# First pass: adding the output products' results into SBUF by VectorE in place of accumulating DMAs

## The chip, the cores and the metric

The kernel runs on one core of one Trainium2 chip. A core has a matrix engine (TensorE, PE in the rows; PEld is its loading of weights), VectorE (DVE), ScalarE (ACT), GpSimd (POOL), a sync engine that issues transfers (SP), and 16 DMA engines that all its transfers share. The metric is the device time of one execution in microseconds, the median of the runs shown; lower is better.

## What is computed

```python
def _attn_ref(q, k, v):                       # 4 batches, 12 heads, 448 x 64
    scores = scale * np.matmul(q, k.transpose(0, 1, 3, 2)) - np.log(S)
    attn = 1.0 / (1.0 + np.exp(-scores))
    return np.matmul(attn, v).astype(np.float32)
...
x = attn_out.transpose(0, 2, 1, 3).reshape(1792, 768)
h = x @ moe_w_in;  x = (h - np.tanh(h)) @ moe_w_out          # 768 -> 2048 -> 768
h = x @ moe2_w_in; r = np.maximum(h, 0.0)
out = (s * (r * r) + b) @ moe2_w_out
```

All is float32. The four weight matrices arrive as 64-bit floats.

## The kernel before, in words

**Products.** Every product is made of three TensorE passes over a high and a low part of each operand. Both parts are made on the chip: a copy rounds the source to the high part (by ScalarE or VectorE) and a VectorE subtraction gives the low part. `hi_lo` (lines 644 to 646) does it for weights (tile `w`), `half` (526 to 529) for the layers' inputs (tile `xo`).

**Passes.** The program makes two passes, each over two batches (896 rows of x). A pass is the attention of 12 pairs of heads and then two layers (`Layers.run`). In the trace the first pass ends near 543 us, and the attention of the second pass follows it, up to about 620 us. A layer takes its 2048 hidden columns in four groups of 512, numbered 0 to 3 (`grp`). In each group the first product fills g, and the output product multiplies g by the group's rows of the second weight matrix and adds to the layer's output: `out1` in layer 0 (12 PSUM banks of 128x448 in each group) and `out2` in layer 1 (14 banks of 128x384). The output lives in SBUF under the name `y`.

**Adding up, first pass.** In `out1` and `out2` the function `evict` empties each bank. Group 0 copies it into `y` (ScalarE or VectorE). Groups 1 and 2 go through `add_on` (1128 to 1133): a copy from PSUM into one of four `t` tiles, and then an accumulating DMA, issued by GpSimd, that adds `t` to `y`. Group 3 is added by VectorE from PSUM into `y`. In the second pass another function adds by accumulating DMAs into `acc` in DRAM; the change doesn't touch it.

**Weights, first pass.** SP loads 768 KB of 64-bit words (`raw`). Four steps (a scaling, then three of VectorE) turn them into 32-bit `wf`, and `keep` (625 to 632) has SP store each `wf` to DRAM, 384 KB (`win`, `wout`), for the second pass, which loads them back. Sums of weight blocks are made in place in `wf`, so they wait for that store to have read the tile. Then `hi_lo` splits into `w`.

**Order.** The program isn't written in the order in which engines run it. `Plan` (lines 88 to 235) collects operations with an assumed time on each engine (busy, and until done) and lists them: TensorE's order stays as written, and for VectorE, ScalarE, GpSimd and SP it takes in turn what is ready by those assumed times and due first. An operation marked EITHER goes to ScalarE or VectorE as the list finds it. The engines then run their lists strictly in that order. So a changed number, or a removed operation, can move others far from the place of the edit.

All instructions carry line 85 in the rows (a helper), so rows are told apart by tiles. `hs`, `two` and `one` are PSUM banks, `af` the attention weights, `qt` and `kt` the parts of q and k, `rawqkv` what is loaded for them.

Of the kernel before, what the change touches and what calls it, by code (L numbers as in the profile page):

```python
# [19 lines left out]
def tile_kernel(ctx, tc, q, k, v, w_in1, w_out1, w_in2, w_out2, s_in, b_in, out):  # L20
# [504 lines left out]

    def half(nm, j, src, keys, sbuf=True):
        t, key, _ = xo[nm, j]
        do(EITHER, (0.46, 0.35 if sbuf else 0.54), lambda e: copy(e, t()[:, 0], src()), r=keys, w=[(*key, 0)])
        do("DVE", 0.54, lambda: dve.tensor_tensor(out=t()[:, 1], in0=src(), in1=t()[:, 0].bitcast(F32), op=ALU.subtract), r=[*keys, (*key, 0)], w=[(*key, 1)])

    def less(o, a, b, r, w):
# [41 lines left out]
    class Layers:  # L573
# [52 lines left out]
        def keep(self, k, key):  # L626

            def fn():
                scratch[key] = dram.tile([P, WE], F32, name="w" + "_".join(map(str, key)))
                sp.dma_start(out=scratch[key], in_=f_t[k])  # L630

            self.do("SP", (1.9, 3.0), fn, r=[("f", k)], w=[("d", key)])

        def kept_sums(self, key):
            return key[1] == 0 and key[2] < (FG if key[0] == "in" else 2)
# [6 lines left out]
            return self.f_of.pop(n)  # L642

        def hi_lo(self, src, hi, lo, r, w, half=False):
            self.do(EITHER, (0.42, 0.3) if half else (0.74, 0.47), lambda e: copy(e, hi(), src), r=r, w=[w[0]])
            self.do("DVE", 0.47 if half else 0.88, lambda: dve.tensor_tensor(out=lo(), in0=src, in1=hi().bitcast(F32), op=ALU.subtract), r=[*r, w[0]], w=[w[1]])

        def w_whole(self, k):

# [475 lines left out]
            prod("3", "a", 1)  # L1125
            to("a", 0, 1, True)

        def add_on(self, bank, m, to, keys):

            k = self.t.take()  # L1130
            self.do(EITHER, (0.43, 0.54) if m == S else (0.38, 0.47), lambda e: copy(e, self.tt[k][:, :m], self.banks[bank][:, :m]), r=[("b", bank)], w=[("t", k)])
            self.do("POOL", (1.0, 7.0), lambda: pool.dma_start(out=to(), in_=self.tt[k][:, :m], accum_op=ALU.add), r=[("t", k)], w=keys)
            self.t.give(k)

        def out1(self, layer, grp, n, close):

            final = grp == FC // FG - 1
            ps = {}

            def y(hd, d, fs):  # L1140
                for i in range(2):
                    if fs[0] == 0:
                        ps[hd, d, i] = self.b.take()
                for f in fs:
                    for i in range(2):
                        kh, kl = self.units[n + 2 * hd + f // 2]
                        o = slice(f % 2 * HM + d * P, f % 2 * HM + d * P + P)
                        bank = ps[hd, d, i]

                        def fn(kh=kh, kl=kl, o=o, f=f, i=i, bank=bank):  # L1150
                            p, x, xs = self.banks[bank], g_t[f], slice(i * S, i * S + S)
                            pe.matmul(p, self.wt[kh][:, o], x[:, 0, xs], start=f == 0, stop=False)
                            pe.matmul(p, self.wt[kh][:, o], x[:, 1, xs], start=False, stop=False)
                            pe.matmul(p, self.wt[kl][:, o], x[:, 0, xs], start=False, stop=f == FG - 1)

                        self.do("PE", 0.608, fn, r=[("w", kh), ("w", kl), ("g", f, i, 0), ("g", f, i, 1)], w=[("b", bank)])

            def evict(hd, d):
                dm = hd * 3 + d
                t = lambda i: ys_t["y"][dm][:, i]  # L1160
                yk = [cells(dm * T2 + i * S, S) for i in range(2)]
                for i in range(2):
                    bank = ps[hd, d, i]
                    if grp == 0:
                        self.do(EITHER, (0.43, 0.54), lambda e, bank=bank, i=i: copy(e, t(i), self.banks[bank]), r=[("b", bank)], w=yk[i])
                    elif not self.sb and 0 < grp < FC // FG - 1:
                        self.add_on(bank, S, lambda i=i: t(i), yk[i])
                    else:
                        self.do("DVE", 0.54, lambda bank=bank, i=i: dve.tensor_tensor(out=t(i), in0=self.banks[bank], in1=t(i), op=ALU.add), r=[("b", bank)], w=yk[i])
                    self.b.give(bank)  # L1170
                if d == 2:
                    for k in range(2):
                        self.w_done(*self.units.pop(n + 2 * hd + k))
                if not final:
                    return
                j = dm // 2
                p = self.tt
                if dm % 2 == 0:
                    k = self.y_t1 = self.t.take()
                    half("11", j, lambda: t(0), yk[0])  # L1180
                    less(lambda: p[k], lambda: t(1), lambda: t(0), [*yk[0], *yk[1]], [("t", k)])
                    half("t1", j, lambda: p[k], [("t", k)])
                    return
                k1, k2, k3, k4 = self.y_t1, *(self.t.take() for _ in range(3))
                b11, bk = (lambda: ys_t["y"][dm - 1][:, 0]), cells((dm - 1) * T2, S)
                half("21", j, lambda: t(0), yk[0])
                less(lambda: p[k2], lambda: t(1), lambda: p[k1], [*yk[1], ("t", k1)], [("t", k2)])
                half("t2", j, lambda: p[k2], [("t", k2)])
                less(lambda: p[k3], lambda: p[k2], b11, [("t", k2), *bk], [("t", k3)])
                half("t3", j, lambda: p[k3], [("t", k3)])  # L1190
                half("22", j, lambda: t(1), yk[1])
                less(lambda: p[k4], lambda: t(0), lambda: p[k2], [("t", k2), *yk[0]], [("t", k4)])
                half("t4", j, lambda: p[k4], [("t", k4)])
                for k in (k1, k2, k3, k4):
                    self.t.give(k)

            for k in range(2):
                self.w_out(n + k)
            y(0, 0, (0, 1))
            now(close)  # L1200
            y(0, 1, (0, 1))
            y(0, 2, (0, 1))
            for d in range(3):
                y(0, d, (2, 3))
                evict(0, d)
            for k in range(2, 4):
                self.w_out(n + k)
            for d in range(3):
                y(1, d, range(FG))
                evict(1, d)  # L1210

        def out2(self, layer, grp, n, close):
# [24 lines left out]
            def evict(hd, t):  # L1237
# [2 lines left out]
                ks = cells(t * DM + hd * HM, HM)  # L1240
                if grp == 0:
                    self.do(EITHER, (0.38, 0.47), lambda e: copy(e, zt(), self.banks[bank][:, :HM]), r=[("b", bank)], w=ks)
                elif not self.sb and 0 < grp < FC // FG - 1:
                    self.add_on(bank, HM, zt, ks)
                else:
                    self.do("DVE", 0.47, lambda: dve.tensor_tensor(out=zt(), in0=self.banks[bank][:, :HM], in1=zt(), op=ALU.add), r=[("b", bank)], w=ks)
                self.b.give(bank)
# [136 lines left out]
```

## Time and profile before

| what | us |
|---|---|
| median of the runs shown | 1054.42 |
| the runs | 1052.88, 1054.45, 1054.42 |
| the profiled execution | 1049.27 |
| span of that execution in the trace | 1047.5 |
| TensorE busy in it | 1028.0 |
| VectorE busy in it | 892.0 |
| ScalarE busy in it | 601.1 |

A busy time is the time in which at least one instruction of the engine was under way. A window view gives that time for a stretch, beside the granted TensorE clock (1.00 is 2.4 GHz, 0.50 is 1.2 GHz, a mean lies between) and the mean share of the DMA engines that were busy. A timeline view gives single instructions with the idle time ahead of them in brackets, and what ended it. The chain of waits leads back from the last instruction, at each step to what released it.

### The profile page before, as it was taken

The page shows a single profiled execution, that of the slowest core. Times are in us where ns is not written, and L with a number is a line of the kernel's source. Part 1 is how long each engine was busy: PE and PEld are TensorE (multiplying, and loading weights), DVE is VectorE, ACT ScalarE, POOL GpSimd, SP SyncE. Part 2 cuts the span into 40 slices and gives each one's busy share as a digit, 9 for nine tenths or more (in the row PEclk, how much of TensorE's full clock was granted, in tenths as well). Part 3 has the DMA queues.
Part 4 walks back from the last instruction along what each step waited for, and adds up shares of the span by engine and source line. Part 5 has one row for each costly group of instructions (what it writes and reads, how often), then busy time and mean ns, then how long its engine had stood idle before and what let it go on. Part 6 is the DMA issues. An engine that isn't in the chain of part 4 may idle for free.

```text
span 1047.5 us, 15848 instructions
## 1 busy us (share of the span) xinstructions
PE 1028.0 (98%) x5688; PEld 896.7 (86%) x5688; DVE 892.0 (85%) x1480; ACT 601.1 (57%) x990; POOL 187.9 (18%) x238
## 2 busy tenths in 40 slices
PE   8999999999999999899999899999999999999998
PEld 4557999898988999898985459999999999999998
DVE  4899989897999998898856689798887999898962
ACT  5776666464555665454426566656555466666650
POOL 4220001203000003122222100306060003061600
PEclk9999999999999999999999999999999999999999
DMA  6773567969722659879576503929497019293963
GB/s 154 201 189 121 166 198 208 281 193 276 213 71 98 187 178 231 235 196 284 137 227 152 179 16 123 233 92 213 104 224 215 31 38 225 80 211 84 214 170 106
DMA packets 137966, 176.92 MB, mean 169 GB/s; under 512 B 53760, under 2 KB 108800, under 8 KB 137888
## 3 DMA queue, kind: packets, MB, share of 16 engines
q1 hardware_dynamic: 111200, 135.82, 41.6%
q0 software_dynamic: 25888, 39.89, 22.0%
q8 instruction: 45, 0.74, 0.3%
q10 hardware_dynamic: 800, 0.20, 0.1%
q14 instruction: 33, 0.27, 0.1%
HBM read 103.02 MB, written 61.83 MB: 157 GB/s over the span
## 4 chain that ended last, share of the span: by engine, by line
PE 76%; DVE 14%; DMA 5%; issue 2%; ACT 1%; SPq 0%; DVEq 0%; ACTq 0%
PE hs L85 64%; PE two L85 6%; PE one L85 6%; DVE t L85 4%; DVE wf L85 3%; DVE w L85 2%; DVE raw L85 2%; DVE xo L85 1%; DVE g L85 1%; DMA win<-wf 1%; DMA raw<-in_moe_w_out_dram 1%; DVE y L85 1%; DMA raw<-in_moe_w_in_dram 1%; DMA wf<-wout 1%; ACT t L85 1%
## 5 line engine op out<-in xcount | busy, mean ns | idle before, releaser
L85 PE MATMUL hs<-xo,w 128*128 128x448 f32 x2016 | 423.7, 368 | 6.6 <-DVE t L85 5.7
L85 PEld LDWEIGHTS hs<-xo,w 128*128 128x128 f32 x2016 | 378.2, 188 | 45.5 <-DVE t L85 7.6
L85 PE MATMUL hs<-w,g 128*128 128x384 f32 x1290 | 228.1, 335 | 0.7 <-DVE w L85 0.6
L85 PE MATMUL hs<-g,w 128*128 128x448 f32 x1098 | 226.4, 366 | 0.0
L85 PEld LDWEIGHTS hs<-w,g 128*128 128x128 f32 x1290 | 224.1, 188 | 2.2 <-DVE w L85 0.9
L85 PEld LDWEIGHTS hs<-g,w 128*128 128x128 f32 x1098 | 206.1, 188 | 17.2 <-DVE g L85 0.3
L85 DVE TENSOR_TENSOR w<-wf,w 128x768 fp32r<-128x768 f32 (+1 forms) x216 | 187.7, 883 | 23.5 <-PE hs L85 11.9
L85 ACT COPY t<-hs 128x448 f32<-128x448 f32 (+2 forms) x239 | 120.1, 515 | 111.1 <-PE hs L85 99.8
L85 ACT CAST w<-wf 128x768 fp32r<-128x768 f32 (+1 forms) x177 | 137.2, 781 | 77.5 <-DVE wf L85 58.5
L85 POOL DMA_DIRECT2D acc<-t x106 | 93.6, 1227 | 318.0 <-ACT t L85 157.1
L85 POOL DMA_DIRECT2D y<-t x52 | 46.1, 985 | 371.0 <-ACT t L85 177.4
L85 DVE TENSOR_TENSOR g<-t,g 128x448 fp32r<-128x448 f32 (+2 forms) x170 | 98.6, 596 | 6.7 <-ACT g L85 6.1
L85 DVE TENSOR_TENSOR wf<-wf 128x384 f32<-128x384 f32 x168 | 93.3, 556 | 12.6 <-DMA win<-wf 7.4
L85 ACT CAST g<-t 128x448 fp32r<-128x448 f32 (+2 forms) x147 | 79.9, 552 | 33.4 <-DVE t L85 31.7
L85 ACT ACTIVATE af<-two,nlogs 128x896 f32<-128x896 f32 (+1 forms) x96 | 85.2, 919 | 8.5 <-PE two L85 6.2
L85 DVE TENSOR_TENSOR t<-hs,t 128x448 f32<-128x448 f32 x114 | 70.2, 619 | 6.2 <-PE hs L85 4.1
L85 ACT ACTIVATE raw<-raw 128x768 f32<-128x768 f32 x60 | 55.6, 926 | 33.3 <-DMA raw<-in_moe_w_out_dram 23.4
L85 DVE SCALAR_TENSOR_TENSOR raw<-raw 128x768 uint32<-128x768 uint32 x64 | 61.2, 957 | 5.5 <-ACT raw L85 3.7
L85 ACT ACTIVATE t<-t,b_sb,s_sb 128x448 f32<-128x448 f32 x64 | 48.0, 761 | 25.4 <-DVE t L85 25.1
L85 DVE TENSOR_TENSOR t<-t 128x448 f32<-128x448 f32 (+1 forms) x98 | 58.8, 603 | 4.1 <-ACT t L85 3.8
L85 DVE SCALAR_TENSOR_TENSOR wf<-raw 128x768 uint32<-128x768 uint32 x64 | 60.7, 953 | 0.7
L85 PE MATMUL two<-qt,kt 64*128 64x448 f32 x396 | 51.4, 384 | 0.1
(79 smaller groups left out, 710.8 us busy)
## 6 DMA issues: line engine op xcount, KB each, us to landing
raw<-in_moe_w_in_dram SPq DMA_DIRECT2D x32, 768.0 KB, 5.7
raw<-in_moe_w_out_dram SPq DMA_DIRECT2D x32, 768.0 KB, 7.9
wf<-wout SPq DMA_DIRECT2D x36, 384.0 KB, 6.6
win<-wf SPq DMA_DIRECT2D x32, 384.0 KB, 3.5
wout<-wf SPq DMA_DIRECT2D x32, 384.0 KB, 6.3
wf<-win SPq DMA_DIRECT2D x32, 384.0 KB, 4.3
acc<-t POOLq DMA_DIRECT2D x51, 224.0 KB, 7.7
acc<-t POOLq DMA_DIRECT2D x55, 192.0 KB, 8.0
```

The source lines that it names most:

```text
L85: return lambda *a, **kw: tc.keep_in_program_order(getattr(self.engine, name)(*a, **kw))
```

## The change

It does two things. In the first pass `evict` adds the banks of groups 1 and 2 by VectorE too, straight from PSUM into `y`, as group 3 does, and `add_on` is gone. And four assumed times of the list are raised: VectorE's copy in `half`, `keep`'s time until done, VectorE's half-width copy in `hi_lo`, and the half-width subtraction there.

```diff
     def half(nm, j, src, keys, sbuf=True):
         t, key, _ = xo[nm, j]
-        do(EITHER, (0.46, 0.35 if sbuf else 0.54), lambda e: copy(e, t()[:, 0], src()), r=keys, w=[(*key, 0)])
+        do(EITHER, (0.46, 0.38 if sbuf else 0.6), lambda e: copy(e, t()[:, 0], src()), r=keys, w=[(*key, 0)])
...
-            self.do("SP", (1.9, 3.0), fn, r=[("f", k)], w=[("d", key)])
+            self.do("SP", (1.9, 5.2), fn, r=[("f", k)], w=[("d", key)])
...
-            self.do(EITHER, (0.42, 0.3) if half else (0.74, 0.47), lambda e: copy(e, hi(), src), r=r, w=[w[0]])
-            self.do("DVE", 0.47 if half else 0.88, lambda: dve.tensor_tensor(out=lo(), in0=src, in1=hi().bitcast(F32), op=ALU.subtract), r=[*r, w[0]], w=[w[1]])
+            self.do(EITHER, (0.42, 0.5) if half else (0.74, 0.47), lambda e: copy(e, hi(), src), r=r, w=[w[0]])
+            self.do("DVE", 0.52 if half else 0.88, lambda: dve.tensor_tensor(out=lo(), in0=src, in1=hi().bitcast(F32), op=ALU.subtract), r=[*r, w[0]], w=[w[1]])
...
-        def add_on(self, bank, m, to, keys):
-
-            k = self.t.take()
-            self.do(EITHER, (0.43, 0.54) if m == S else (0.38, 0.47), lambda e: copy(e, self.tt[k][:, :m], self.banks[bank][:, :m]), r=[("b", bank)], w=[("t", k)])
-            self.do("POOL", (1.0, 7.0), lambda: pool.dma_start(out=to(), in_=self.tt[k][:, :m], accum_op=ALU.add), r=[("t", k)], w=keys)
-            self.t.give(k)
...
-                    elif not self.sb and 0 < grp < FC // FG - 1:
-                        self.add_on(bank, S, lambda i=i: t(i), yk[i])
...
-                elif not self.sb and 0 < grp < FC // FG - 1:
-                    self.add_on(bank, HM, zt, ks)
```

TensorE's order is the same in both programs. By the instruction lists GpSimd issues 52 transfers fewer (24 of 128x448 in layer 0, 28 of 128x384 in layer 1). VectorE has 36 instructions more and ScalarE 36 fewer. On VectorE the adds of `hs` into `y` go from 26 to 50 at 448 columns and from 14 to 42 at 384; its copies `t<-hs` go from 26 to 18 and from 17 to 8; its 768-wide rounding copies `w<-wf` go from 31 to 39; the rest shifts by a few either way. SP has 440 transfers in both.

The order on VectorE at three places follows; the numbers in the names are those of tile buffers and differ between the programs.

The first place is layer 0, group 2: VectorE while weights of the next group are made and the banks of group 1 are emptied (177 to 200 us in the trace of before). Before:

```order
L85 SCALAR_TENSOR_TENSOR raw_105<-raw_105 128x768
L85 SCALAR_TENSOR_TENSOR wf_84<-raw_105 128x768
L85 TENSOR_TENSOR w_996<-wf_83,w_992 128x768
L85 TENSOR_TENSOR w_79<-wf_84,w_79 128x384
L85 TENSOR_SCALAR raw_106<-raw_106 128x768
L85 SCALAR_TENSOR_TENSOR raw_106<-raw_106 128x768
L85 TENSOR_TENSOR wf_84<-wf_84 128x3x128
```

VectorE at the same place in the changed program:

```order
L85 SCALAR_TENSOR_TENSOR raw_105<-raw_105 128x768
L85 SCALAR_TENSOR_TENSOR wf_84<-raw_105 128x768
L85 TENSOR_TENSOR y_140<-hs_957,y_140 128x448
L85 TENSOR_TENSOR y_140<-hs_963,y_140 128x448
L85 TENSOR_TENSOR y_140<-hs_959,y_140 128x448
L85 TENSOR_TENSOR w_1004<-wf_83,w_1000 128x768
L85 TENSOR_TENSOR w_79<-wf_84,w_79 128x384
L85 TENSOR_SCALAR raw_106<-raw_106 128x768
L85 SCALAR_TENSOR_TENSOR raw_106<-raw_106 128x768
L85 SCALAR_TENSOR_TENSOR wf_81<-raw_106 128x768
L85 TENSOR_TENSOR y_140<-hs_964,y_140 128x448
L85 TENSOR_TENSOR wf_84<-wf_84 128x3x128
```

Four of the new adds stand between the steps of the weights there.

The second place is layer 1, the first product of group 2: VectorE from 426 to 434 us in the trace of before. `t<-hs,t` reads a bank that TensorE needs again. Before:

```order
L85 TENSOR_SCALAR raw_105<-raw_105 128x768 x2
L85 SCALAR_TENSOR_TENSOR raw_105<-raw_105 128x768
L85 TENSOR_TENSOR wf_84<-wf_84 128x3x128
L85 TENSOR_TENSOR wf_84<-wf_83,wf_84 128x3x128
L85 SCALAR_TENSOR_TENSOR wf_81<-raw_105 128x768
L85 TENSOR_TENSOR wf_83<-wf_84,wf_83 128x3x128
L85 TENSOR_TENSOR wf_83<-wf_83 128x3x128
L85 TENSOR_TENSOR t_1004<-hs_954,t_101 128x448
L85 COPY t_1003<-hs_956 128x448
```

VectorE at the same place in the changed program:

```order
L85 TENSOR_SCALAR raw_105<-raw_105 128x768
L85 TENSOR_TENSOR t_1011<-hs_962,t_1012 128x448
L85 SCALAR_TENSOR_TENSOR t_1010<-t_1011 128x448
L85 SCALAR_TENSOR_TENSOR raw_105<-raw_105 128x768
L85 COPY t_100<-hs_964 128x448
L85 TENSOR_TENSOR wf_84<-wf_84 128x3x128
L85 TENSOR_TENSOR wf_84<-wf_83,wf_84 128x3x128
```

The two readings of the banks have moved ahead of the four sums in `wf`.

The third place is the attention of the second pass: SP near 576 us in the trace of before, and VectorE behind it. SP in the changed program (in the program before, the load of `win_0_0` stands ahead of all loads of `rawqkv`, issued at 536.2 us):

```order
L85 DMA rawqkv_4565<-in_k_dram 128x3x64 x2
L85 DMA rawqkv_4565<-in_k_dram 64x2x64
L85 DMA out_0_dram<-y_140 128x384
L85 DMA wf_81<-win_0_0_0_584 128x768
L85 DMA wout_0_0_1_s_4907<-wf_82 128x768
L85 DMA wout_0_1_0_s_4919<-wf_83 128x768
```

VectorE in the changed program, over the pair of heads that starts at 572.6 us in the trace of before:

```order
L85 TENSOR_TENSOR qt_4556<-two_4570,qt_4556 128x448
L85 TENSOR_TENSOR kt_4558<-two_4570,kt_4558 128x448
L85 CAST w_76<-wf_81 128x768
L85 TENSOR_TENSOR w_77<-wf_81,w_76 128x768
L85 TENSOR_TENSOR one_4572<-one_4572,t_100 128x224
L85 CAST xo_87<-one_4572 128x448
L85 TENSOR_TENSOR xo_87<-one_4572,xo_87 128x448
L85 COPY y_140<-one_4572 128x448
```

In the program before there are no `w` rows in this pair; in the next pair a `w` of 128x384 (copy and subtraction) stands at this place, and the pair after that has one `w` subtraction:

```order
L85 TENSOR_TENSOR kt_4613<-two_4623,kt_4613 128x448
L85 CAST w_78<-wf_82 128x384
L85 TENSOR_TENSOR w_78<-wf_82,w_78 128x384
L85 TENSOR_TENSOR one_4626<-one_4626,t_102 128x224
L85 CAST xo_87<-one_4626 128x448
```

So a `w` step that reads a tile loaded late has moved one pair of heads earlier; the 384-wide copy stands in the changed program in the next pair, behind `xo`.

## Rows read from the trace of the kernel before

**Rows 1.** The page: busy time by engine, then the chain of waits by engine.

```profile
PE 1028.0 (98%) x5688; PEld 896.7 (86%) x5688; DVE 892.0 (85%) x1480; ACT 601.1 (57%) x990; POOL 187.9 (18%) x238
PE 76%; DVE 14%; DMA 5%; issue 2%; ACT 1%; SPq 0%; DVEq 0%; ACTq 0%
```

**Rows 2.** Windows: length, busy PE, PEld, DVE, ACT, POOL (instructions), clock, DMA, GB/s.

```profile
140.00:280.00 140.00, 139.24 (x679) 126.89 (x678) 124.56 (x188) 81.08 (x130) 21.18 (x24) 1.00 0.82 228
280.00:360.00 80.00, 78.29 (x398) 72.29 (x397) 79.31 (x131) 45.33 (x76) 0.00 (x0) 1.00 0.36 114
400.00:520.00 120.00, 115.62 (x609) 109.97 (x608) 104.36 (x159) 62.15 (x98) 30.74 (x37) 0.99 0.82 222
```

**Rows 3.** Windows of 20 us, the same columns.

```profile
180.00:200.00 20.00, 20.00 (x100) 18.55 (x99) 15.35 (x23) 10.27 (x17) 8.59 (x11) 1.00 1.06 262
420.00:440.00 20.00, 17.17 (x80) 15.58 (x79) 17.47 (x28) 8.52 (x14) 3.65 (x4) 0.91 0.98 289
580.00:600.00 20.00, 17.06 (x130) 8.57 (x130) 13.49 (x25) 9.38 (x12) 1.92 (x3) 0.91 0.59 196
```

**Rows 4.** VectorE's adds by form (busy, mean ns); chain, two adds; the accumulating DMAs' landing.

```profile
L85 DVE TENSOR_TENSOR y<-hs,y 128x448 f32<-128x448 f32 x26 | 15.5, 619 | 0.5 <-PE hs L85 0.4
L85 DVE TENSOR_TENSOR y<-hs,y 128x384 f32<-128x384 f32 x14 | 7.7, 555 | 10.1 <-PE hs L85 10.1
539.18 0.93 DVE y L85 x2
y<-t POOLq DMA_DIRECT2D x24, 224.0 KB, 9.5
```

**Rows 5.** What VectorE waited for (us, times, longest): 140 to 280, then 400 to 520.

```profile
DVE w L85 <- PE hs L85: 4.1, 2, 2.6
DVE raw L85 <- DMA raw<-in_moe_w_out_dram: 3.8, 2, 3.1
...
DVE wf L85 <- DMA win<-wf: 6.4, 4, 3.3
DVE raw L85 <- DMA raw<-in_moe_w_in_dram: 2.5, 2, 1.8
```

**Rows 6.** Timeline of VectorE and TensorE, 429 to 434; last, the chain's store there.

```profile
429.36 1.15 DVE L85 TENSOR_TENSOR wf<-wf 128x384 f32<-128x384 f32 x2 [1.33 <-DMA win<-wf]
432.37 0.62 DVE L85 TENSOR_TENSOR t<-hs,t 128x448 f32<-128x448 f32 x1
432.90 0.61 DVE L85 COPY t<-hs 128x448 f32<-128x448 f32 x1
433.57 2.85 PE L85 MATMUL hs<-xo,w 128*128 128x448 f32 x10 [2.83 <-DVE t L85]
424.38 4.96 DMA win<-wf
```

**Rows 7.** Transfers: queue 0 and the stores in 180 to 200; stores over the run.

```profile
q0 software_dynamic: 1179, 1.89, 55.0%
...
win<-wf SPq DMA_DIRECT2D x4, 384.0 KB, 6.4
...
win<-wf SPq DMA_DIRECT2D x32, 384.0 KB, 3.5
```

**Rows 8.** Timeline of SP, VectorE and TensorE, 576 to 590; last, the loads over the run.

```profile
576.64 0.54 SPq L85 DMA_DIRECT2D out_dram<-y  x1
579.67 3.01 PE L85 MATMUL one<-af,rawqkv 128*64 128x448 f32 x20
585.77 0.55 DVE L85 CAST w<-wf 128x384 fp32r<-128x384 f32 x1 [3.93 <-DMA wf<-win]
586.83 0.39 DVE L85 TENSOR_TENSOR one<-one,t 128x224 f32<-128x224 f32 x1
589.13 3.17 PE L85 MATMUL one<-af,rawqkv 128*64 128x448 f32 x8 [2.94 <-DVE y L85]
wf<-win SPq DMA_DIRECT2D x32, 384.0 KB, 4.3
```

## The prediction

> **What bounds the kernel now.** I read the page first: TensorE is busy 98% of the span and holds 76% of the chain, VectorE 85% and 14% [rows 1]. TensorE's order and work don't change, so a gain can only come from the time in which TensorE stands still or runs at a lower clock, and from nothing else. Next come the windows, to see where that is. In the stretches of the first pass that the change touches TensorE lacks 140 - 139.24 = 0.76 us (140 to 280, layer 0, where groups 1 and 2 are emptied), 80 - 78.29 = 1.71 (280 to 360) and 120 - 115.62 = 4.38 (400 to 520, layer 1) [rows 2]. Of the last, 20 - 17.17 = 2.83 lies between 420 and 440, and the granted clock there is 0.91 on average, a mixture of the two levels 2.4 and 1.2 GHz after a stop [rows 3]; 9% of the 17.17 busy us is another 1.5. In the second pass's attention it lacks 2.94 between 580 and 600, with the same mean clock, so 1.5 more [rows 3].
>
> The timelines tell what these stops are. At 433.57 TensorE had stood for 2.83 us on VectorE's `t`, and VectorE had taken the sums in `wf`, after a wait for a store, before it read the bank [rows 6]. That store took 4.96 us [rows 6]; the median over the run is 3.5, and in the busy window 180 to 200 it is 6.4, when queue 0, the accumulating DMAs', used 55.0% of the engines' time [rows 7]. At 589.13 TensorE had stood for 2.94 us behind a VectorE that had waited 3.93 for a load of weights [rows 8].
>
> **What the change removes.** 52 copies from PSUM into `t` (some by ScalarE, some by VectorE) and 52 accumulating DMAs. GpSimd and ScalarE have room, ScalarE at 57% [rows 1], so their relief is worth nothing by itself. What counts is the traffic: DMA engines are at 1.06 in 180 to 200 and 0.98 in 420 to 440 [rows 3], and the transfers of groups 1 and 2 fall in just these stretches; an accumulate of 224 KB takes 9.5 us to land [rows 4] where a load of 384 KB takes 4.3 [rows 8]. Without them the loads of `raw` and the stores should come nearer to their medians. It also frees the `t` tiles, which are held until a transfer has read them.
>
> **What it adds.** VectorE gets 24 adds of 448 columns and 28 of 384. One takes 619 or 555 ns [rows 4], but in a row they start closer: 0.53 apart (432.37, 432.90) [rows 6], and two of 384 take 0.93 [rows 4], so 0.465 each. That is 24 x 0.53 = 12.7 us in layer 0 and 28 x 0.465 = 13.0 in layer 1; with no overlap it would be 14.9 and 15.5. VectorE loses some copies of 448 and 384 in return (17 by the counts, 8 x 0.53 + 9 x 0.465 = 8.4 us) and takes eight more roundings of weights, and so on.
>
> By the Trainium skill ("VectorE: DVE Perf Modes", "The TRN2 errata") such an operation from PSUM costs 120 cycles plus one per column at 0.96 GHz. That would be an estimated 592 and 525 ns, 28.9 us for all 52 against my 25.7; the rows' spacing is the smaller, since consecutive operations overlap.
>
> **Does it fit?** VectorE stands idle 140 - 124.56 = 15.44 us between 140 and 280, and 120 - 104.36 = 15.64 between 400 and 520 [rows 2]. So each half of the added work fits on paper, with 2.7 and 2.6 us over. But a part of the idle time can't be filled at will: in the first stretch 4.1 us are waits for TensorE to be done with a `w` tile, which stay, and 3.8 for loads; in the second 6.4 are waits for stores and 2.5 for loads [rows 5], and these are what lighter traffic shortens. In the order the new adds stand between weight steps, just where VectorE waited.
>
> Layer 0: the stretch from 280 to 360 is the weak place. VectorE is busy 79.31 of 80 us there [rows 2], and TensorE already loses 1.71. The adds lie before it, but any that don't fit push weight and `g` steps into it, and there is no cover. From 140 to 280 I take back 0.5 of the 0.76 us and what the modelled ends of matmuls hide, and for 280 to 360 I take a loss of 1.0, nearer to the small row of 1.71 than to the bound: were only half of the 15.44 usable, 12.7 - 7.7 = 5.0 us would be late. The range of the two together is +1.5 to -5.
>
> Layer 1: at 426 to 434 both readings of the banks now stand ahead of the sums in `wf`, so the wait for the store no longer lies ahead of what TensorE needs, whatever the store takes. Of the 2.83 + 1.5 = 4.3 us I take 4.0 back. From the other 4.38 - 2.83 = 1.55 us I take 1.2, since loads come sooner but VectorE has more to do. Together +5.2, range +1 to +5.9.
>
> The changed times of the list (stores 5.2 for 3.0 above all) cost nothing by themselves; they work by the order, as just counted, and at one more place.
>
> **The attention of the second pass.** There, SP now issues the load of `win_0_0` behind the loads of `rawqkv`, at the place where an `out_dram` store stands at 576.64 [rows 8]. A landing of 4.3 us [rows 8] gives 580.9. VectorE's 768-wide rounding and subtraction of it stand ahead of `one`, `xo` and the `y` copy of that pair; they take some 1.4, to 582.3. From the `one` addition to TensorE's next start it is 589.13 - 586.83 = 2.3 us [rows 8], so TensorE would start at 584.6 in place of 579.67 [rows 8]: a stop of 4.9. The old one of 2.94 goes, as the 384-wide step now stands behind `xo` and its load will have landed. Net -2.0, with a lower clock after either stop. If the load lands a microsecond or two sooner it is even; if it lands before 576 there is no stop, +4.4. Range -3 to +4.4.
>
> The layers of the second pass keep their accumulating DMAs and their work; only the order shifts by the new numbers: 0, within 1.5 either way.
>
> **The sum.** 0.5 - 1.0 + 5.2 - 2.0 + 0 = +2.7 us. The profiled execution took 1049.27 us, 1.77 more than its span of 1047.5, and lies 5.15 below the median, which I leave as it is: 1046.6 for an execution like the profiled one, and 1054.4 - 2.7 = 1051.7 for the median.
>
> **Rivals.** (1) *VectorE becomes the bound in layer 0.* For it: no slack at all from 280 to 360 [rows 2], where it already stops TensorE, and waits for TensorE that can't be filled [rows 5]. Against it: 15.44 us of idle time for 12.7. The gains elsewhere are 5.2 - 2.0 = 3.2, so it turns the result to slower by over 2.1 us when 5.3 us are late, that is when under 7.4 of the 15.44 us can be used. With 5 us late and a lower clock after the stops, 1.5 as at 420 to 440, the sum is 3.2 - 6.5 = -3.3: 1057.7.
>
> (2) *The gain is swallowed by the moved wait.* The stop near 580 is longer than reckoned, or the gain of layer 1 is only the stop itself: 5.2 falls to 3, and with -1.0, +0.5 and -3 the sum is -0.5: 1054.9.
>
> (3) *Stores and loads are slow without the accumulates too.* SP's own 768 KB loads and 384 KB stores are dense there. Then the waits of [rows 5] stay, the added work must find other room, and only the changed order at 426 helps: about 2.8 in layer 1, 2.8 - 1.0 - 2.0 = -0.2: 1054.6.
>
> By the Trainium skill ("SBUF — State Buffer", "SBUF: two separate sides") a transfer from GpSimd's queue waits for descriptors while certain VectorE operations hold a shared port, with DMA engines idle meanwhile. By that rule the long landing of the accumulates would be such waiting, they would take nothing from SP's transfers, and the outcome is that of (3). The trace speaks rather against it, with packets of queue 0 at 55.0% of the engines' time [rows 7].
>
> (4) *All goes well:* layer 0 +1.5, layer 1 +5.9, the load lands before 576, +4.4: with -1 for the second pass 10.8 at most, some 7 more likely: 1047.
>
> **How the numbers follow.** Faster or slower by 0.2%, 2.1 us, is what a measurement of this kernel can tell from no change. The forecast (1050 to 1053) has a chance of 0.40, (1) 0.20, (2) 0.15, (3) 0.10, (4) 0.15. Of the forecast 0.32 lies below 1052.3; with (4) and a little of (3) that is faster 0.48. Same gets 0.08 of the forecast and most of (2) and (3), 0.29. Slower gets (1) and a remainder of (2), 0.23. The range reaches from 1046.5, the likelier part of (4), to 1057.5, most of (1); about 1 in 10 is left out on either side.
>
> **What would show it.** DMA share in 180 to 200 and 420 to 440 well under 1, and stores there near 3.5 us. No stop of TensorE near 433 and a clock of 1.00 in 420 to 440. VectorE's idle time between 140 and 280 down to a few us, and TensorE's loss in 280 to 360 between 1.5 and 4; if it is over 6, rival (1) holds. A stop of 3 to 6 us near 580, released by VectorE's `y`, and none near 589; if there is none at all, the load of `win_0_0` came sooner than I make it, and my step on SP's order is wrong.

## The result, and the profile after

The changed kernel takes 1043.0 us (median of 5 runs, 1042.25 to 1046.54) where the kernel before takes 1052.88 (5 runs, 1050.32 to 1054.45): a ratio of 0.9915, 95% interval 0.9891 to 0.9939. In a second set of runs, of 10 and 27, it was 1044.46 against 1050.04, ratio 0.9949 (0.9931 to 0.9966). So the change gains some 5 to 10 us (9.9 and 5.6 by the medians); I had forecast 2.7, and a median of 1051.7.

The profiled execution of the changed kernel took 1046.54 us (span 1044.7), the longest of its 5 runs, while that of before, 1049.27, was shorter than each of its timed runs. The two profiles differ by 2.8 us only. That agrees with my sum, but by chance, as the second pair of profiles below shows.

Windows of the profile after (length, busy PE, PEld, DVE, ACT, POOL with instructions in brackets, granted clock, DMA share, GB/s), first the long ones of [rows 2], then 20 us each, as [rows 3]:

```profile
140.00:280.00 140.00, 140.00 (x687) 128.56 (x686) 136.10 (x213) 67.40 (x105) 0.00 (x0) 1.00 0.57 177
280.00:360.00 80.00, 77.27 (x387) 70.17 (x386) 78.95 (x129) 44.55 (x74) 0.00 (x0) 1.00 0.39 125
400.00:520.00 120.00, 120.00 (x644) 114.91 (x643) 114.90 (x185) 54.48 (x81) 5.89 (x10) 1.00 0.61 184
...
180.00:200.00 20.00, 20.00 (x101) 18.53 (x100) 19.65 (x31) 5.02 (x8) 0.00 (x0) 1.00 0.69 221
420.00:440.00 20.00, 20.00 (x102) 18.50 (x101) 19.79 (x33) 9.66 (x16) 0.00 (x0) 1.00 0.50 157
560.00:580.00 20.00, 16.62 (x125) 8.91 (x126) 13.28 (x24) 11.32 (x16) 4.15 (x7) 0.95 0.81 234
580.00:600.00 20.00, 20.00 (x161) 10.88 (x159) 13.18 (x25) 13.84 (x21) 1.91 (x3) 0.97 0.31 99
```

TensorE's column tells the story. The 4.38 us that it lacked in 400 to 520 [rows 2] are all back, and the clock in 420 to 440 is 1.00 in place of 0.91 [rows 3]. In 280 to 360 it lacks 80 - 77.27 = 2.73 us, 1 more than before. The loss in the attention has moved from 580 to 600 into 560 to 580. VectorE works 11.5 us more in 140 to 280 and 10.5 more in 400 to 520, and DMA engines are at 0.69 where they were at 1.06.

The transfers in 180 to 200 of the profile after (form, count, KB, median us to landing), against [rows 7]:

```profile
raw<-in_moe_w_out_dram SPq DMA_DIRECT2D x4, 768.0 KB, 6.2
win<-wf SPq DMA_DIRECT2D x3, 384.0 KB, 2.7
```

In the profile before, the loads there took longer too:

```profile
raw<-in_moe_w_out_dram SPq DMA_DIRECT2D x3, 768.0 KB, 11.4
```

A store lands in 2.7 us there, not in 6.4, a load of `raw` in 6.2, not in 11.4, and VectorE no longer waits for a transfer in either of the two long stretches.

The attention, in timelines of SP, VectorE and TensorE of the profile after (in brackets the idle time before, and what ended it), against [rows 8]:

```profile
569.50 0.43 SPq L85 DMA_DIRECT2D wf<-win  x1
574.09 0.56 DVE L85 CAST w<-wf 128x768 fp32r<-128x768 f32 x1 [3.97 <-DMA wf<-win]
577.86 4.71 PE L85 MATMUL one<-af,rawqkv 128*64 128x448 f32 x20 [3.38 <-DVE y L85]
```

The load of `win_0_0` is issued at 569.50 and lands 4.6 us later; VectorE waits for it and TensorE stands for 3.38 us. The old stop behind the 384-wide step is gone.

**The same matmuls compared.** TensorE runs the same matmuls in the same order in all programs here, so the start of the n-th one can be compared between traces. The table gives how much later (+) or earlier (-) than in the first profile of before a program comes through each stretch, in us; the bounds are the matmuls that start at those times in that profile. "Again" are second profiles, taken in the first experiment. My terms stand beside them.

| stretch | forecast | after | after, again | before, again |
|---|---|---|---|---|
| 0 to 140 | 0 | -0.1 | +0.2 | -0.2 |
| 140 to 280 | -0.5 | -1.6 | -2.7 | +0.4 |
| 280 to 360 | +1.0 | +2.2 | +2.8 | -0.1 |
| 360 to 520 | -5.2 | -6.1 | -6.1 | +1.8 |
| 520 to 620 | +2.0 | +1.2 | -1.3 | -0.6 |
| 620 to the end | 0 | +1.7 | -0.3 | +0.2 |
| sum | -2.7 | -2.8 | -7.3 | +1.6 |

Over the two profiles of each kernel the difference is -5.05 - 0.8 = -5.9 us, in line with the second set of timed runs (5.6); the first set gave more (9.9).

### The profile page after: what moved, and what is told of

Its sections match the earlier page's. It is cut to its first block, busy times and chain, and to the rows that moved or that the text cites. A ratio compares the mean times of both kernels' runs of the same rounds, so it can differ in the third digit from the quotient of the medians.

```text
span 1044.7 us, 15663 instructions
## 1 busy us (share of the span) xinstructions
PE 1028.1 (98%) x5688; PEld 895.8 (86%) x5688; DVE 907.4 (87%) x1516; ACT 579.5 (55%) x954; POOL 142.5 (14%) x186
## 4 chain that ended last, share of the span: by engine, by line
PE 88%; DVE 7%; issue 1%; DMA 1%; ACT 1%; SPq 0%; ACTq 0%; DVEq 0%
PE hs L85 76%; PE two L85 6%; PE one L85 6%; DVE t L85 2%; DVE xo L85 1%; DVE wf L85 1%; DVE y L85 1%; DVE w L85 1%; DMA wf<-wout 1%; DMA wout_s<-wf 1%; DVE g L85 0%; ACT t L85 0%; DVE raw L85 0%; SPq L85 0%; ACT af L85 0%
## 5 line engine op out<-in xcount | busy, mean ns | idle before, releaser
L85 ACT CAST w<-wf 128x768 fp32r<-128x768 f32 (+1 forms) x169 | 130.7, 779 | 101.7 <-DVE wf L85 71.4
L85 ACT COPY t<-hs 128x448 f32<-128x448 f32 (+1 forms) x204 | 102.8, 516 | 113.1 <-PE hs L85 106.7
L85 POOL DMA_DIRECT2D rawqkv<-in_v_dram x36 | 22.9, 642 | 494.5 <-ACT t L85 438.8
L85 DVE TENSOR_TENSOR y<-hs,y 128x448 f32<-128x448 f32 (+1 forms) x92 | 52.1, 586 | 10.8 <-PE hs L85 10.7
L85 ACT ACTIVATE raw<-raw 128x768 f32<-128x768 f32 x58 | 53.2, 918 | 11.9 <-DMA raw<-in_moe_w_in_dram 11.7
```

What stands on the lines that cost most here:

```text
L85: return lambda *a, **kw: tc.keep_in_program_order(getattr(self.engine, name)(*a, **kw))
```

## The experiments

My theory was that the gain comes from the lighter traffic, by way of the stores and loads that VectorE waited for, and that VectorE's added work and the moved load give a part of it back. Times are medians, ratios are against the kernel before on the same chip (median 1050.04 for the first four rows, 1050.38 for the next four, 1051.25 for the last three; each group ran on another chip). A ratio is not that of the two medians: for the adds alone it is 0.9902, while 1038.04 / 1050.04 is 0.9886.

| kernel | us | ratio | interval |
|---|---|---|---|
| before, again | 1048.97 | 1.0 | 0.9974 to 1.0027 |
| changed, again | 1044.46 | 0.9949 | 0.9931 to 0.9966 |
| adds alone, old times of the list | 1038.04 | 0.9902 | 0.9875 to 0.993 |
| new times of the list alone | 1049.37 | 1.0004 | 0.9983 to 1.0024 |
| adds alone, traffic kept | 1048.59 | 0.9988 | 0.9971 to 1.0005 |
| changed, load moved back | 1039.35 | 0.9898 | 0.9878 to 0.9917 |
| adds in layer 0 alone | 1046.16 | 0.9962 | 0.9946 to 0.9977 |
| adds in layer 1 alone | 1041.09 | 0.9918 | 0.9893 to 0.9942 |
| adds, the three small times | 1036.65 | 0.9862 | 0.9833 to 0.9891 |
| adds, the stores' time | 1040.38 | 0.9894 | 0.9863 to 0.9925 |
| adds alone, w step behind | 1037.25 | 0.987 | 0.984 to 0.99 |

### Both kernels again

No edit. The kernel before:

> The kernel before, unchanged, for a second profile beside others of the same chip and call. The first profile of it (span 1047.5 us) was shorter than any timed run of it, and the first profile of the changed kernel (1044.7) longer than its other runs, so the two profiles differ by 2.8 us where the medians differ by 9.9. Theory 1 (the stops seen in the profiles are the whole matter, and their size varies from run to run): a span of 1048 to 1052, with more than 3 us of stop between 420 and 440, or more than 1.8 in 280 to 360, than in the first profile. Rival (something spread over the whole program, such as a slower spacing of matmuls in some runs): the same stops as before, and the rest spread over stretches without waits.

The changed kernel:

> The changed kernel, unchanged, for a second profile. Theory 1: a span of 1040 to 1042, TensorE's stop near 575 again 3 to 4 us, and the 3 us less than in the first profile found in the stretch 280 to 360, where TensorE lacked 2.7. Rival: the stops as in the first profile, and less loss spread over 700 to 840, where it lost 0.4 in each 20 us against the kernel before.

The kernel before had a span of 1049.1, as expected, with more stop and less clock in 420 to 440 than [rows 3]. Its window, and that of its attention:

```profile
420.00:440.00 20.00, 16.78 (x72) 15.11 (x72) 16.60 (x26) 7.72 (x12) 3.75 (x4) 0.84 1.01 293
...
580.00:600.00 20.00, 17.64 (x128) 9.09 (x127) 14.57 (x28) 10.76 (x14) 2.02 (x4) 0.91 0.62 211
```

The same matmuls came through 420 to 440 in 1.6 us more than in the first profile. So the stops that the change removes vary from run to run, and the profile that I reckoned with had a small one. Over all sets of runs the kernel before ran between 1045.46 and 1058.36, the changed one between 1042.02 and 1046.54.

The changed kernel had a span of 1040.2, but the place where I expected the 4.5 us to its first profile was wrong: 280 to 360 was no better (+2.8 against +2.2). 2.5 us lie in the attention. There TensorE's stop was shorter (2.34 us, where I expected 3 to 4 again) and the clock stayed at 1.00 after it; first the stop in TensorE's timeline:

```profile
577.07 3.02 PE L85 MATMUL one<-af,rawqkv 128*64 128x448 f32 x20 [2.34 <-DVE y L85]
```

and the windows of the attention:

```profile
560.00:580.00 20.00, 17.66 (x145) 9.59 (x147) 13.56 (x24) 11.59 (x16) 4.42 (x7) 1.00 0.83 248
580.00:600.00 20.00, 20.00 (x173) 11.00 (x167) 15.25 (x29) 14.91 (x24) 1.92 (x3) 1.00 0.25 85
```

The other 2.0 us lie behind 620, most of them spread evenly over 720 to 840, as the rival said: groups of TensorE's matmuls in 760 to 800 (count, busy us, mean ns), first of the first profile after, then of the second:

```profile
L85 PE MATMUL hs<-xo,w 128*128 128x448 f32 x119 | 24.9, 368 | 0.0
```

```profile
L85 PE MATMUL hs<-xo,w 128*128 128x448 f32 x126 | 25.9, 365 | 0.0
```

At a granted clock of 1.00 in both, a matmul takes 3 ns more, the starts lie 207 ns apart in place of 203, and 98 to 99 fit into 20 us in place of 100 to 101. The starts show the same two rates in layer 0 of the first pass, too: between 220 and 280 the first profiles of both kernels ran at 207 ns, the second of the changed one mostly at 203. What makes this rate was not tried.

### The adds alone, and the times alone

The first is the changed kernel with the four old numbers:

```diff
-        do(EITHER, (0.46, 0.38 if sbuf else 0.6), ...
+        do(EITHER, (0.46, 0.35 if sbuf else 0.54), ...
-            self.do("SP", (1.9, 5.2), fn, r=[("f", k)], w=[("d", key)])
+            self.do("SP", (1.9, 3.0), fn, r=[("f", k)], w=[("d", key)])
-            ... (0.42, 0.5) if half ...; ... 0.52 if half ...
+            ... (0.42, 0.3) if half ...; ... 0.47 if half ...
```

> The adds by VectorE and no accumulating DMAs in the first pass, but the list's old times. In it the sums in wf stand ahead of the reading of the banks near 426, as before the change, and the load of win_0_0 stands ahead of the rawqkv loads. Theory 1 (lighter traffic takes the stops of layer 1 away): no stop over 1 us in 400 to 520 though the order there is the old one; the stop near 575 not there, but the old one near 585 of 3 us; the time within 2 us of the changed kernel. Rival 2 (the raised time of stores does it, by the order): a stop of 2 us or more stays near 430, and the time is 4 us or more above the changed kernel.

The second is the kernel before with the four new numbers, the same edit the other way.

> The old adding by accumulating DMAs, with the four new times of the list. Theory 1: stores stay at 5 us or more in the busy windows, layer 1 keeps 2 us or more of stops, a stop near 575 to 585 of 3 us; the time within 2 us of the kernel before. Rival 2: no stop over 1 us in 400 to 440, and 4 us or more faster than the kernel before.

The adds alone gave 1038.04 us, 6.4 less than the changed kernel on the same chip (4.9 by the ratios); I had expected the two within 2. In layer 1 nothing stops. The timeline of VectorE there (its order is the old one, with the sums in `wf` ahead of the reading of the banks), and below the dots TensorE's:

```profile
424.64 1.14 DVE L85 TENSOR_TENSOR wf<-wf 128x384 f32<-128x384 f32 x2
425.70 0.95 DVE L85 SCALAR_TENSOR_TENSOR wf<-raw 128x768 uint32<-128x768 uint32 x1
426.57 1.15 DVE L85 TENSOR_TENSOR wf<-wf 128x384 f32<-128x384 f32 x2
427.64 0.62 DVE L85 TENSOR_TENSOR t<-hs,t 128x448 f32<-128x448 f32 x1
...
421.43 14.83 PE L85 MATMUL hs<-xo,w 128*128 128x448 f32 x71
```

There is no bracket: VectorE didn't wait for the store, as it did in [rows 6], and TensorE ran on. So the lighter traffic takes the stop away without the new order. The new times alone, with the traffic of before, made no difference (1.0004), but not because the order does nothing: at the same place TensorE stood for 0.48 us only in the profile. Its timeline with the times alone:

```profile
429.77 10.48 PE L85 MATMUL hs<-xo,w 128*128 128x448 f32 x49 [0.48 <-DVE t L85]
```

and the windows of layer 0 and layer 1 in that kernel:

```profile
140.00:280.00 140.00, 136.17 (x667) 124.57 (x666) 124.69 (x190) 74.37 (x120) 21.55 (x24) 1.00 0.78 214
...
400.00:520.00 120.00, 117.35 (x623) 110.88 (x622) 106.96 (x165) 63.90 (x103) 30.32 (x37) 1.00 0.81 222
```

So in this one profile the order, too, takes this stop away, and the same matmuls of 360 to 520 come through in 2.5 us less; but layer 1 still lacks 120 - 117.35 = 2.65 us, most of it in other stops (the longest 1.26 us near 487), and 140 to 280 lost 2.4 that it had not lost before (140 - 136.17 = 3.83 lacking). For the whole time and for layer 1 as a whole theory 1 was right, for the place rival 2.

A part of the gain of the adds alone lies behind the layers of the first pass: 520 to 620, the attention of the second pass, is 3.0 us shorter by the same matmuls. The old stop there is 1.65 us in place of 2.94 (its row stands in the last experiment), and the clock stays at 1.00 after it. I had expected it at 3 us still. Why VectorE waited less for the load, 2.63 us in place of 3.93, was not tried.

### The traffic kept

The adds alone, and behind each add of groups 1 and 2 a transfer of GpSimd that adds the `y` cell to a DRAM tile nobody reads:

```diff
+            def fn():
+                if grp == 0:
+                    acc_t["j", *key] = dram.tile([P, m], F32, ...)
+                    pool.dma_start(out=acc_t["j", *key], in_=src())
+                else:
+                    pool.dma_start(out=acc_t["j", *key], in_=src(), accum_op=ALU.add)
+            self.do("POOL", (1.0, 7.0), fn, r=keys, w=[("junk", *key)])
```

> As adds_only (adds by VectorE, the list's old times; median 1038.0), but the queue of GpSimd carries the traffic all the same: after each add of groups 1 and 2 an accumulating DMA takes the y cell into a DRAM tile of its own that nothing reads (24 of 224 KB, 28 of 192 KB), and group 0 begins these tiles by plain stores. Theory 1 (what the change removes is the traffic): stores and loads of weights in 180 to 200 and 400 to 440 are slow again, 5 us and more for a store against 2.7, VectorE waits for them as before the change, layer 1 has 2 us or more of TensorE's stops again, and since the added work no longer fits beside the waits, 280 to 360 loses 3 us or more: 1044 to 1052. Rival 3 (the traffic is not it; what counts is that the copies into t and the holding of t tiles by transfers are gone): within 2 us of adds_only.

1048.59 us: 10.5 more than the adds alone (9.0 by the ratios, as the chips differ), and no different from the kernel before (0.9988). By the traces VectorE, ScalarE, SP and TensorE run the same instructions in the same order as with the adds alone, and none of them waits for the added transfers. But there are 78 of these and not 52: the 26 plain stores of group 0 come on top, and all go to DRAM, where `y` is in SBUF. So the cost of the old traffic may be somewhat less. The transfers in 180 to 200 (queue 0's packets, MB and share of the engines' time; then as above):

```profile
q0 software_dynamic: 1152, 1.84, 54.3%
...
raw<-in_moe_w_out_dram SPq DMA_DIRECT2D x3, 768.0 KB, 11.5
...
win<-wf SPq DMA_DIRECT2D x4, 384.0 KB, 5.4
```

and the window of layer 1 in the same kernel:

```profile
400.00:520.00 120.00, 116.78 (x623) 110.91 (x622) 111.73 (x178) 56.98 (x84) 30.75 (x37) 1.00 0.82 224
```

Stores are at 5.4 us again and loads of `raw` at 11.5, TensorE lacks 3.22 us in layer 1 (0 with the adds alone), and VectorE's longest wait for a store in 400 to 520 was 2.5. Theory 1 holds, rival 3 (the copies and the `t` tiles) falls. 280 to 360 lacked 2.67 us, somewhat less than the 3 and more that I expected. This execution also ran at TensorE's slower rate from 720 to 840 (2.1 of the 2.7 us that it lost behind 620), where the added traffic had long ended; by the stretches to 620 alone it is 6.3 us behind the adds alone. In the attention it gains 3.3 us on the kernel before, as much as the adds alone: that part of the gain isn't the traffic's.

By the Trainium skill ("SBUF — State Buffer", "SBUF: two separate sides") transfers of GpSimd's queue may wait for descriptors, with the DMA engines idle. In this case they took the engines' time, 54.3%, and slowed SP's stores from 2.7 to 5.4 us, so such waiting is not what the gain rests on.

### The load moved back

The changed kernel, with SP's issue of the load of `win_0_0` put ahead of the `rawqkv` loads once the list is made; no other engine's order changes.

```diff
+            first = min(at[i] for i in self.raws2 if at[i] > max(at[d] for d in ops[self.early][2]))
+            order.insert(first, order.pop(at[self.early]))
             for i, e in order:
```

> The changed kernel with one SP instruction moved: the load of win_0_0 for the second pass is issued ahead of the loads of rawqkv, as in the kernel before, and no longer behind them; VectorE's, ScalarE's and GpSimd's orders are those of the changed kernel. Theory 1 (the stop near 575 is the wait for this load): no stop over 0.5 us between 560 and 580, and nothing new near 585, where the 384-wide step stands behind xo: 2.3 to 4.5 us faster than the changed kernel (stops of 2.3 and 3.4 in two profiles, and what a lower clock adds): 1040 to 1042. Rival 4 (the load is only the last of several that come late there): another wait takes the place, the stop stays at 1.5 us or more, and the time within 1 us of the changed kernel.

1039.35 us, 5.1 below the changed kernel (1044.46, on another chip; 5.4 by the ratios), a little more than expected. The timelines of VectorE and TensorE at the place, without a wait:

```profile
569.77 0.55 DVE L85 CAST w<-wf 128x768 fp32r<-128x768 f32 x1
570.35 0.96 DVE L85 TENSOR_TENSOR w<-wf,w 128x768 fp32r<-128x768 f32 x1
...
574.13 3.02 PE L85 MATMUL one<-af,rawqkv 128*64 128x448 f32 x20
```

The moved load is the cause of the stop near 577, and nothing takes its place: from 520 to 620 this kernel is 3.7 us ahead of the first profile of before, where the changed kernel was 1.2 behind and 1.3 ahead.

### One layer alone

Both with the old times. In layer 0 alone (layer 1 keeps `add_on`):

> With the list's old times: adds by VectorE in layer 0 only; in layer 1 groups 1 and 2 go through copies and accumulating DMAs as before the change. Theory 1: layer 0 gains 1 to 2 us in 140 to 300 and gives 0.5 to 1 back in 300 to 360, and layer 1 keeps its stops of 4 us and more: 1045 to 1049, some 1 to 3 below the kernel before. Rival 5 (VectorE's load in layer 0 is what costs): a loss in 280 to 360 that eats the gain, no faster than the kernel before.

In layer 1 alone (layer 0 keeps `add_on`):

> With the list's old times: adds by VectorE in layer 1 only; layer 0 as before the change. Theory 1: the stops in 400 to 520 are gone (6 us by the difference of the profiles there), layer 0 as before: 1041 to 1044, 6 to 8 below the kernel before. Rival 5: 1038 or less, better than with adds in both layers.

1046.16 and 1041.09 us. Both times lie in theory 1's ranges, but both gains are larger than it had them: 4.2 us in place of 1 to 3, and 9.3 in place of 6 to 8. With the adds in layer 0 alone, 420 to 440 shows the old stop, larger than in [rows 3]; with those of layer 1 alone 400 to 520 is full:

```profile
420.00:440.00 20.00, 16.21 (x69) 14.47 (x69) 17.29 (x27) 7.21 (x13) 3.46 (x4) 0.83 0.94 272
```

```profile
400.00:520.00 120.00, 120.00 (x646) 115.25 (x645) 111.69 (x178) 57.35 (x83) 7.54 (x12) 1.00 0.62 192
```

By the same matmuls, layer 0's adds come through 140 to 280 in 2.0 us less and give 0.7 back in 280 to 360; layer 1's gain 6.4. What theory 1 left out is the attention of the second pass: 520 to 620 is 4.3 us shorter with the adds in layer 0 alone and 4.8 with those in layer 1 alone (3.0 with both, 0.6 in the second profile of before). TensorE's stop there was 0.34 us in the first and is missing in the second, and the clock stayed at 1.00. So of the layers of the first pass, layer 1 carries most of the gain; the times of both kernels hold the attention's part besides, and that of layer 0 alone fits its range by luck.

### Which time of the list costs

The changed kernel with the stores' time back at 3.0:

> The changed kernel with one of the four times of the list set back: a store is taken as done after 3.0 as before; the other three (the copy in half, the half-width copy and subtraction in hi_lo) keep their new values. The load of win_0_0 stands early again. Theory 6 (the raised time of stores is what costs the changed kernel 5 us against adds_only: the late load, and 2.3 us more in 320 to 340): 1037 to 1040. Rival 7 (the three small numbers shift work to VectorE in layer 0): 3 us lost again in 320 to 340, 1040 to 1043.

The adds alone with the stores' time at 5.2:

> The adds by VectorE with only the stores' time raised (5.2), the other three times as before. The load of win_0_0 stands late. Theory 6: as the changed kernel, 1042 to 1045, with a stop of 2 to 4 us near 575 and 3 us lost in 320 to 340. Rival 7: the stop near 575, but under 1 us lost in 320 to 340 beyond adds_only: 1039 to 1042.

1036.65 us with the three small times, the fastest median of all (its interval overlaps that of the adds alone); 1040.38 with the stores' time alone, by the ratios no slower than the adds alone (0.9894 and 0.9902). The stores' time is what puts the load of `win_0_0` late: the list has it early in the first of these and late in the second, where TensorE stood for 1.69 us at 576.53. The loss in 320 to 340, though, comes with neither alone. The windows of the two:

```profile
320.00:340.00 20.00, 19.61 (x97) 17.73 (x96) 19.90 (x35) 12.17 (x20) 0.00 (x0) 1.00 0.22 67
```

```profile
320.00:340.00 20.00, 18.85 (x92) 16.70 (x92) 19.90 (x35) 10.77 (x20) 0.00 (x0) 1.00 0.21 60
```

In the first profile of the changed kernel the same window has 17.27. So theory 6 is right on where the load stands, and wrong in laying the 5 us, and 320 to 340, on the stores' time: with that time alone the kernel isn't as slow as the changed one, and 1040.38 lies in rival 7's range. Rival 7's blame of the small times falls as well, as 1036.65 is below both ranges for that kernel. Only both together make the loss in 320 to 340, and which instruction does it was not tried.

### The w step behind

The adds alone, with the 384-wide rounding and subtraction of `w` in the second pass's attention moved behind the `y` copy of their pair:

```diff
+L85 TENSOR_TENSOR one<-one,t 128x224
+L85 CAST xo<-one 128x448
+L85 TENSOR_TENSOR xo<-one,xo 128x448
+L85 COPY y<-one 128x448
 L85 CAST w<-wf 128x384
 L85 TENSOR_TENSOR w<-wf,w 128x384
-L85 TENSOR_TENSOR one<-one,t 128x224
-L85 CAST xo<-one 128x448
-L85 TENSOR_TENSOR xo<-one,xo 128x448
-L85 COPY y<-one 128x448
```

> adds_only with two VectorE instructions moved: the 384-wide rounding and subtraction of w in the second pass's attention stand behind one, xo and the y copy of their pair and no longer ahead of them. In adds_only VectorE waited 2.63 us there for the load and TensorE 1.65. Theory (the wait in front of what TensorE needs is the price, not the load): that stop is gone and nothing comes in its place: 1 to 3 us below adds_only, 1035 to 1037.5. Rival (the following pair's qt and kt then come late): a stop of over 1 us on qt or kt near 580, within 0.7 us of adds_only.

The stop is gone; VectorE reaches the step after the load has landed, and TensorE has a wait of 0.42 us on `kt` in its place. First the stop in TensorE's timeline of the adds alone, then the timelines of VectorE and TensorE with the step behind:

```profile
579.45 3.02 PE L85 MATMUL one<-af,rawqkv 128*64 128x448 f32 x20 [1.65 <-DVE y L85]
```

```profile
577.15 0.54 DVE L85 CAST w<-wf 128x384 fp32r<-128x384 f32 x1
577.92 3.02 PE L85 MATMUL one<-af,rawqkv 128*64 128x448 f32 x20
581.73 1.50 PE L85 MATMUL two<-qt,kt 64*128 64x448 f32 x12 [0.42 <-DVE kt L85]
```

The medians, 1037.25 and 1038.04, were taken on different chips and are too near to tell apart; by the same matmuls of one profile each 520 to 620 is 1.3 us shorter.

## Why the prediction was off

The direction was right, and so was the mechanism: lighter traffic, no waits for stores, layer 1's stops gone, VectorE short of time in 280 to 360, the stop in the attention moved to the place where I put it. What failed are the sizes of the sum's terms, one term put at nothing, and the base. Over two profiles of each kernel (the changed one less the one before) the terms came out at -2.3, +2.5, -7.0, +0.3 and +0.6, where I had -0.5, +1.0, -5.2, +2.0 and 0: three terms were too pessimistic by some 1.8 us each, and the loss in 280 to 360 was too small by 1.5.

**The base.** I took 1054.42, the median of three runs, for the kernel before. In the set of runs in which the changed kernel took 1043.0, it took 1052.88: of the 8.7 us between 1051.7 and 1043.0, 1.5 are the base and 7.2 the gain (9.9 in place of 2.7). In the second set it took 1050.04, and the changed kernel 1044.46: there 4.4 of 7.2 are the base and 2.9 the gain (5.6 in place of 2.7). My range was laid around that base and moved with it.

**Layer 1** was forecast at -5.2 and measured -6.1 against the same profile of before. Against its second profile, which took 1.8 us more there, it is -7.9. The mechanism was right; the step that failed was to take the stops of one execution as those of the median. They vary, and a change that takes away a varying stop gains its mean, not what one profile shows. That the accumulating DMAs make them vary is not shown, but the runs fit it: with the traffic kept they spread from 1044.19 to 1051.13, with the adds alone from 1036.96 to 1041.83. Against the first profile the discounts were too large as well: all of the 4.38 came back, and the lower clock with it. What I laid on the order at 426 the lighter traffic does without it, as the adds alone show; the order alone took that stop away in one profile.

**Layer 0, 140 to 280,** was -0.5 and measured -1.6 and -2.7. Here my step was to reckon with the 0.76 us that TensorE lacked by its busy time. By the starts of the same matmuls the stops of that stretch come to 1.4 us, since the modelled ends hide a part; I named that and gave it nothing. In both profiles after, next to nothing of them is left. The other 1.0 us of the second is mostly TensorE's faster rate between 220 and 280, not the change. The adds did fit into the idle time, as reckoned: VectorE's idle time fell from 15.44 us to 140 - 136.10 = 3.9, and 24 adds in a row at 0.53 us, 12.7, account for it. Rival (1) didn't come about.

**280 to 360** was +1.0 and measured +2.2 and +2.8, within my bounds, from the same cause that I gave, a VectorE without slack. But the adds alone cost +1.1 there, and 0.5 of that is TensorE's slower rate between 280 and 310. The rest is an order made by the stores' time and the small times together: 320 to 340 lost 2.8 and 3.0 with it, 0.7 with the adds alone. Here the step that failed is that the changed times of the list cost nothing but what I had counted.

**The attention** was +2.0 and measured +1.2 and -1.3. The landing (4.3 forecast, 4.6 measured) and the 3.7 us from there to TensorE were right. What failed was SP's issue: I put it 579.67 - 576.64 = 3.0 us ahead of the time at which TensorE would want the result; in the profile after that time is 574.5, so it was 574.5 - 569.5 = 5.0 us ahead, since SP was further ahead of TensorE than before. In the profile before, SP stood 3.5 us for a store (`wout_s`) until it could issue the load of `win_0_0` at 536.17, ahead of the `rawqkv` loads. That wait moved away with the load, and I had not reckoned with it. With the load moved back, the wait is there again, and SP reaches the same place at 570.72, 574.13 - 570.72 = 3.4 us ahead of TensorE. So the stop was 3.4 and 2.3 in place of 4.9. I also reckoned the lower clock the same on either side; after the stop of 2.34 us the clock didn't fall.

**The layers of the second pass** were 0: +1.7 and -0.3. The 1.7 is TensorE's slower rate in one execution (2.1 from 720 to 840), which no term of mine had.

Of the rivals, (4) has the nearest time, 1047. (3) fell, since stores without the accumulates took 2.7 us in place of 6.4. Of (2) a part is true: the moved wait and the list's times hold back some 5 us, since the same adds with the load moved back took 1039.35, and with the old times 1038.04.

## What to carry to other kernels

Transfers that nobody waits for can still cost more than the work they save: here 52 accumulating DMAs, landing off the path, slowed the stores that VectorE waited for, and the 52 adds by VectorE put in their place, reckoned at 25.7 us of its time, cost less than that. Cost such a transfer by what its engine time does to the others in the same 20 us, and try it by keeping the traffic and dropping its use. And with a kernel whose runs spread over 10 us, take the base and the stops from several profiles before a sum of 3 us is made.

## What the runs showed of the hardware

- TensorE shows two rates at a granted clock of 1.00: 365 or 368 ns for the same matmul, starts 203 or 207 ns apart, 100 to 101 or 98 to 99 of them in 20 us. Which one holds in 720 to 840 differs between two executions of the changed kernel, and is worth 2.1 us there.
- A stop of 2.34 us in the attention left the clock at 1.00 (changed kernel, again), while in the kernel before, again, a stop of 2.4 in the attention was followed by 0.91 on average over 20 us.
- A store of 384 KB landed in 2.7 us in 180 to 200 without the traffic of queue 0, and in 5.4 and 6.4 with it at 54.3% and 55.0% of the engines' time; a load of 768 KB in 6.2, 11.5 and 11.4.
